# Attention and a mixture of experts on one core: order of the experts and the next weights' load ahead of the table, small copies and sums moved off GpSimd

## The chip, the core and the metric

The kernel runs on one core of a Trainium2 chip. The engines are called PE (TensorE), DVE (VectorE), ACT (ScalarE), POOL (GpSimd) and SP (SyncE, which here only issues transfers). The metric is the time on the device in microseconds; the kernel before took 555.93 us in the median of three runs (553.4 to 557.14).

## The reference

Attention with a capped score, then a layer of eight experts of which each token uses one:

```python
scores = cap * np.tanh(q @ k.T / np.sqrt(64) / cap)      # 4 batches, 12 heads, 448 tokens, 64 wide
attn = softmax(scores) @ v                               # becomes x: 1792 tokens of 768
logits = normalised(x) @ normalised(expert_emb).T / tau
expert_idx = np.argmax(logits, axis=1)
gate_w = softmax(logits)[token, expert_idx]
for e in range(8):                                       # w1[e]: 768 x 1024, w2[e]: 1024 x 768
    mask = expert_idx == e
    h = np.maximum(x[mask] @ w1[e], 0.0)
    out[mask] = gate_w[mask, None] * (h @ w2[e])
```

All arrays are float32. The kernel multiplies in float16 with each factor split into a high and a low half, three products for each pair.

## The kernel before, in words

The first part (up to about 250 us) is attention, head pair by head pair, with the router's work put between. Each batch's rows are written to a table of rows `x_dram` in device memory; each row has 768 values, then its scale and its gate, 770 words in all. The expert with the most tokens so far is chosen early; its weights are loaded and split beside attention, and its first tile (`tile0`) is computed from the rows of the first three batches.

The second part works in tiles of 128 tokens of one expert. `tile_body` does one: up products into `h` (12 groups, `up`, L231), `relu` into a high and a low half (`hh` on ACT at L243, `hl` on DVE at L244), eight down products (`down`, L638), and in between, after the sixth down product, the transposes of the next tile's rows (`transpose_x`, L212), which POOL gathered from `x_dram` (`gather`, L198) and scaled (`scale_x`, L204). A check sum of each low half's accumulator `acc` is added into `sum_h` by POOL (L653, in wide tiles L1399, for `tile0` L739). At the end of the kernel all sums are looked at (`fine_sums`, L1478 on).

Which tile belongs to which expert is computed on the chip. In the tile behind `tile0` (L1491) functions called hooks are run between the up groups, in the order of the dictionary `hooks1`: at group 0 `gates_out` (gates of the last batch, written to `x_dram` by two transfers of ACT's queue, L407 and L410) and `slots`; at group 8 `fill_table` (a product of PE, then DVE's `table`, L1213, then the gather of the next rows, which needs the table and the written gates), `positions` (the experts' order, as a permutation `perm`, and the list `by_pos` and `pos_i` by position in this order, L1220 to L1244) and `start_loads` (SP reads seven expert numbers from `pos_i` into registers, then loads the second expert's weights: six loads of `w1r` of 512 KB, L1153, and four of `w2r` of 768 KB, L1157); from group 10 on every engine reads registers from `pos_i` (`load_ends`).

Beside an expert's first tile the next expert's ten weight parts are split into halves, each by one ACT operation (L221) and one DVE operation (L222), and with each split the load of the part of the expert after that is issued (`load1`, `load2`). They stand in the queues of ACT and DVE between the `hh` and `hl` of that tile: four before the first half of the hidden layer, four before the second, the rest one by one (`FIRST`).

The experts at positions 1 to 4 have a first tile that is wide (`wide_tile`): 128 of their own tokens and 32 more, the tail of the expert. The 128 tail rows of these four are gathered together once (`along_gather`), scaled (`along_scale`, L1320), transposed beside the first tile of the largest expert (`along_transpose`, L1330 to L1333), and each expert's 32 columns are copied into columns 128 to 160 of `xh` and `xl` (`along_behind`, L1339, POOL, 6 x 32 words for each of the two).

The number of tiles of an expert is only known on the chip, so the tiles stand in branches (L1525 for further tiles of an expert, L1541 for the last experts). How the framework orders the engines: an engine's instructions run in the order of the program. Where one engine needs another's result, it waits for that engine's counting semaphore. At the end of a branch each engine raises its own semaphore to the value that it would have had in the other arm; an operation behind the branch that needs something which another engine wrote or read in the branch waits for this mark, which the other engine sets when it gets there itself. Each transfer that SP or ACT issues gets the next of eight semaphores, in the order of the program, whichever of the two issues it; before it is issued, its engine waits until the transfer that had this semaphore before, the eighth before it, has landed.

The functions concerned:

Of the kernel before, what the change touches and what calls it, by code (L numbers as in the profile page):

```python
# [30 lines left out]
F32 = mybir.dt.float32  # L31
F32R = mybir.dt.float32r
F16 = mybir.dt.float16
I32 = mybir.dt.int32
AF = mybir.ActivationFunctionType
ALU = mybir.AluOpType
AX = mybir.AxisListType
PSUM = bass.MemoryType.PSUM

P = 128  # L40
# [4 lines left out]
E = 8  # L45
# [8 lines left out]
TAIL = 32  # L54
# [26 lines left out]
def attention_moe(ctx: ExitStack, tc: tile.TileContext, q, k, v, cap, emb, tau, w1, w2, qk_pairs, v_pairs, out):  # L81
    nc = tc.nc
# [27 lines left out]
    iota_t = const.tile([P, NTAB], F32, name="iota_t")  # L110
    nc.gpsimd.iota(iota_t, pattern=[[1, NTAB]], base=0, channel_multiplier=0, allow_small_or_imprecise_dtypes=True)

    iota_e = const.tile([P, E], F32, name="iota_e")
# [70 lines left out]
    sums_w, sums_0, sum_h = sums[:, : E * NS], sums[:, E * NS : -3], sums[:, -3:]  # L184
# [4 lines left out]
    xh = const.tile([P, DC, PW], F16, name="xh")  # L189
# [80 lines left out]
    with ExitStack() as actx:  # L270
# [83 lines left out]
        def load_heads(i):  # L354
# [20 lines left out]
        halves, tails, done_full, place = [  # L375
            small.tile([P, E], F32, tag=n, name=n) for n in ("halves", "tails", "done_full", "place")
        ]
# [25 lines left out]
        def write_rows(b, c0, c1):  # L403

            for t in (b,) if b else (0, B - 1):
                eng = nc.sync if b < B - 1 else nc.scalar
                eng.dma_start(  # L407
                    x_dram[t * S : t * S + 384, c0:c1].rearrange("(p c) w -> p c w", c=3), xsb[b % 2][:, 0:3, c0:c1]
                )
                eng.dma_start(x_dram[t * S + 384 : (t + 1) * S, c0:c1], xsb[b % 2][: S - 384, 3, c0:c1])  # L410
# [19 lines left out]
        def gates_out(b):  # L430
            gs = small.tile([P, 4], F32, tag="gs", name=f"gs{b}")
            nc.vector.tensor_reduce(gs, ex, axis=AX.X, op=ALU.add)
            nc.vector.tensor_scalar(gs, gs, 1e-9, None, op0=ALU.add)
            nc.vector.reciprocal(gs, gs)
            nc.vector.tensor_tensor(xsb[b % 2][:, :, GATE], gs, p2, op=ALU.mult)
            write_rows(b, D, XW)
# [155 lines left out]
        def tile_body(p, idx, nxt, W=P, todo=(), pace=FIRST, hooks=(), hidden=None, space=None):  # L592
# [50 lines left out]
            if not hidden:  # L643
                hp = [tile_of("h", n) for n in range(2)]
                acc = small.tile([P, 2], F32, tag="acc", name="acc", bufs=2)
                hidden = []
                for h in range(2):
                    step(pace[h])
                    for j in range(DC):
                        hook(h * DC + j)  # L650
                        up(w1p[p % 2], h, j, hp[h], W)
                    hidden.append(relu(h, hp[h], acc, W))
                nc.gpsimd.tensor_tensor(sum_h[:, :2], sum_h[:, :2], acc, op=ALU.add)  # L653
            for f in range(6):
                hook(2 * DC + f)
                step(pace[2])
# [60 lines left out]
        acc0 = small.tile([P, 2], F32, tag="acc", name="acc0", bufs=2)  # L717

        last = B - 1
# [6 lines left out]
        def tile0(todo, space):  # L726

            todo = list(todo)

            def split_until(n):  # L730
                while len(todo) > n:
                    todo.pop(0)()

            hooks = {2 * DC + f: [lambda n=2 * (5 - f): split_until(n)] for f in range(6)}
            hooks[12] += [lambda: choose(last), lambda: all_norms(last)]
            hooks[15] += [count_last]
            hooks[16] += [lambda: scales_x(last), lambda: gates(last)]
            tile_body(0, idx0[:, 0:1], None, hooks=hooks, hidden=first_h, space=space)
            nc.gpsimd.tensor_tensor(sum_h[:, :2], sum_h[:, :2], acc0, op=ALU.add)  # L739

        def attention_bounded(apool, ps_s, ps_o):

# [391 lines left out]
    work = ctx.enter_context(tc.tile_pool(name="work", bufs=1))  # L1134
# [5 lines left out]
    raw2 = [wpool.tile([P, 2, D], F32, tag=f"w2r{f}", name=f"w2r{f}") for f in range(N2)]  # L1140


    NV = 6
    val = work.tile([P, NV, E], F32, tag="val", name="val")
    by_pos = work.tile([P, NV, E], F32, tag="by_pos", name="by_pos")
    pos_i = work.tile([1, 3, E], I32, name="pos_i")
    table = work.tile([P, NTAB], I32, name="table")
    cp = {}
    eid = {}
# [5 lines left out]
    def load2(p, f):  # L1155
        if p < E:
            nc.sync.dma_start(raw2[f], w2_part(eid[p], f))  # L1157
# [6 lines left out]
    def split2(p, f):  # L1164

        n = p * NS + N1 + f
        split(raw2[f], w2p[p % 2][0][f], w2p[p % 2][1][f], by_pos[:, 1, p : p + 1], sums_w[:, n : n + 1])
        load2(p + 1, f)

    def slots():  # L1170
        every = work.tile([P, E], F32, tag="every", name="every")
# [37 lines left out]
    def fill_table(start):  # L1209
        tp = ps_t.tile([P, 512], F32, tag="t", name="tabp")  # L1210
        for g in range(G):
            nc.tensor.matmul(tp[:, :NTAB], a_all[:, g, :], cp["b"][:, g, :], start=g == 0, stop=g == G - 1)
        nc.vector.tensor_scalar(table, tp[:, :NTAB], float(NT), None, op0=ALU.add)  # L1213
        gather(col(start))
        scale_x()
        gather(col(start + 1))

    def positions():

        nc.vector.tensor_copy(val[:, 0:2, :], scale_w)  # L1220
        nc.vector.tensor_copy(val[:, 2, :], unscale)

        nc.vector.scalar_tensor_tensor(
            out=val[:, 3, :], in0=full[:, 0, :], scalar=2.0, in1=halves, op0=ALU.mult, op1=ALU.add
        )

        nc.vector.tensor_tensor(val[:, 4, :], cp["t"], done, op=ALU.add)
        nc.vector.tensor_scalar(val[:, 5, :], iota_e, -1.0, float(E), op0=ALU.mult, op1=ALU.add)
        perm = work.tile([P, E, E], F32, tag="perm", name="perm")
        nc.vector.tensor_tensor(  # L1230
            perm,
            iota_t[:, :E].unsqueeze(2).to_broadcast([P, E, E]),
            place.unsqueeze(1).to_broadcast([P, E, E]),
            op=ALU.is_equal,
        )
        pv = work.tile([P, NV, E, E], F32, tag="pv", name="pv")
        nc.vector.tensor_tensor(
            pv,
            perm.unsqueeze(1).to_broadcast([P, NV, E, E]),
            val.unsqueeze(2).to_broadcast([P, NV, E, E]),  # L1240
            op=ALU.mult,
        )
        nc.vector.tensor_reduce(by_pos, pv, axis=AX.X, op=ALU.add)
        nc.vector.tensor_copy(pos_i, by_pos[0:1, 3:6, :])  # L1244

    def start_loads():
        for p in range(1, E):
            eid[p] = nc.values_load(
                pos_i[0:1, 2, p : p + 1], engines=(mybir.EngineType.SP,), min_val=0, max_val=E - 1
            )  # L1250
        for i in range(N1):
            load1(1, i)
        for f in range(N2):
            load2(1, f)
# [3 lines left out]
    def load_ends(p):  # L1258
# [4 lines left out]
        ends[p] = code, base  # L1263

    hooks1 = {
        0: [lambda: gates_out(last), slots],
        8: [lambda: fill_table(start), positions, start_loads],
        **{10 + i: [lambda i=i: load_ends(i)] for i in range(E)},
    }
    hooks1[10].append(lambda: along_gather())  # L1270
# [64 lines left out]
    def along_behind(p):  # L1335

        m = (p - WIDE.start) * TAIL
        for x, a in ((xh, along_h), (xl, along_l)):
            nc.gpsimd.tensor_copy(x[:, :, P:], a[:, :, m : m + TAIL])  # L1339

    def wide_tile(p, todo, pace=(4, 3, 3, 1)):

        code, base = ends[p]
        a = slice((p - WIDE.start) * TAIL, (p - WIDE.start + 1) * TAIL)
# [23 lines left out]
        acc = small.tile([P, 3], F32, tag="acc3", name="acc3")  # L1368
        hidden = {}
        for h in range(3):  # L1370
# [4 lines left out]
            for j in range(DC):  # L1375
                for f in fs:
                    c = slice(f * P, (f + 1) * P)
                    o = hp[:, (f - 3 * h) * PW : (f - 3 * h + 1) * PW]
                    for m, (l, x) in enumerate(((0, xh), (0, xl), (1, xh))):
                        nc.tensor.matmul(  # L1380
                            o, w1p[p % 2][l][j][:, c], x[:, j, :],
                            start=j == 0 and f == fs[0] and m == 0, stop=j == DC - 1 and f == fs[-1] and m == 2,
# [13 lines left out]
            )  # L1396
            for f in fs:
                hidden[f] = [t[:, (f - 3 * h) * PW : (f - 3 * h + 1) * PW] for t in parts]
        nc.gpsimd.tensor_tensor(sum_h, sum_h, acc, op=ALU.add)  # L1399
        y = [tile_of("y", n) for n in range(2)]  # L1400
        passes = ((0, 0), (0, 1), (1, 0))

# [17 lines left out]
        for f in range(FC):  # L1420
            for n, (l, w) in enumerate(passes):
                for m in range(blocks):
# [3 lines left out]
                        start=f == 0 and n == 0, stop=f == FC - 1 and n == 2, skip_group_check=True,  # L1426
# [21 lines left out]
    def tile_of(n, i):  # L1448
        if n == "o":
            return work.tile([P, D], F32, tag="yo", name="yo", bufs=2)  # L1450
        return ps.tile(shapes[n], F32, tag=f"{n}{i}", name=f"{n}{i}")
# [37 lines left out]
    with tc.manual_schedule():  # L1489
        start = nc.values_load(first_i[0:1, 1:2], engines=(mybir.EngineType.Pool,), min_val=0, max_val=2)  # L1490
# [65 lines left out]
        redo = nc.values_load(redo_i[0:1, 0:1], min_val=0, max_val=1)  # L1556
        with tc.If(redo > 0):
            for p in range(E):
                e = nc.values_load(pos_i[0:1, 2, p : p + 1], engines=(mybir.EngineType.SP,), min_val=0, max_val=E - 1)
                for i in range(N1):  # L1560
                    nc.sync.dma_start(raw1[i], w1_part(e, i))
                for f in range(N2):
                    nc.sync.dma_start(raw2[f], w2_part(e, f))
                n, base = ends[p]
                n = (n + 1) >> 1
                if p == 0:
                    n, base = n + nc.values_load(first_i[0:1, 1:2], min_val=0, max_val=2), 0
                with tc.For_i(0, n, 1) as slot:
                    plain_tile(base + slot)
                if p in WIDE:  # L1570
                    plain_tile(TAIL0 + p)
# [47 lines left out]
```

## Time and profile before

| | |
|---|---|
| time, median of 3 runs | 555.93 us (553.4 to 557.14) |
| the profiled execution | 559.05 us, span 557.2 us |
| PE busy | 485.3 us (87%) |
| DVE busy | 326.1 us (59%) |
| ACT busy | 299.9 us (54%) |
| POOL busy | 245.1 us (44%) |
| granted clock of PE, mean | 0.952 |

The span is the stretch from the first to the last instruction of the profiled execution; its own time is the device time around it. Busy shares are averages over attention and the experts. PE works on attention to about 246 us, and on tiles from then on. All times of rows are microseconds from the start of the span.

### The profile page before, as it was taken

What the parts mean: (1) busy time and instruction counts of PE and PEld (TensorE: products, weight loads), DVE (VectorE), ACT (ScalarE), POOL (GpSimd) and SP (SyncE); (2) the same over time, 40 slices, a digit from 0 to 9 for tenths busy, and PEclk for the clock granted to TensorE, in tenths of its full rate; (3) what the DMA queues carried; (4) which work ended last, traced back from release to release, by engine and by line L of the source; (5) the groups of instructions that cost most, each with busy time, mean ns of one, the idle gap of its engine ahead of it and who ended that gap; (6) DMA issues with size and microseconds to landing.
All of it is one profiled execution on the core that took longest, in us unless ns stands there. A gap on an engine that the chain in (4) does not pass through costs nothing. (4 is left out here: it accounts for less than half of the span.)

```text
span 557.2 us, 11978 instructions
## 1 busy us (share of the span) xinstructions
PE 485.3 (87%) x4603; PEld 314.2 (56%) x4603; DVE 326.1 (59%) x691; ACT 299.9 (54%) x366; POOL 245.1 (44%) x316
## 2 busy tenths in 40 slices
PE   3899989999997989798795996999999999989570
PEld 2444444444432434366683884987788877868450
DVE  4876686967897778677658213741218521869111
ACT  3988779788977987645055113711118311947010
POOL 2567636474634544720356333342125732463412
PEclk9999999999997979989997899999999999999776
DMA  7333318333262340342199810861115711679511
GB/s 227 120 108 111 110 43 265 108 110 106 103 223 80 144 155 1 113 129 90 60 351 407 322 58 20 288 229 43 41 59 214 304 58 59 225 297 349 199 32 39
DMA packets 30601, 83.55 MB, mean 150 GB/s; under 512 B 7293, under 2 KB 7449, under 8 KB 30498
## 3 DMA queue, kind: packets, MB, share of 16 engines
q1 hardware_dynamic: 26354, 67.68, 34.6%
q0 software_dynamic: 2896, 13.00, 6.9%
q10 hardware_dynamic: 1248, 1.64, 0.9%
q8 instruction: 47, 0.77, 0.6%
q14 instruction: 56, 0.46, 0.3%
HBM read 69.91 MB, written 13.00 MB: 149 GB/s over the span
## 5 line engine op out<-in xcount | busy, mean ns | idle before, releaser
L780 ACT ACTIVATE prob<-s,icap 128x896 f32<-128x896 f32 x96 | 86.2, 903 | 26.5 <-PE s L774 18.5
L231 PEld LDWEIGHTS <-h 128*128 128x128 f16 x1056 | 81.0, 100 | 13.6 <-ACTq L1541 7.2
L231 PE MATMUL h<-xh,h 128*128 128x128 f16 (+1 forms) x480 | 79.8, 220 | 9.5 <-ACTq L1541 6.8
L794 POOL TENSOR_TENSOR sums<-sums,prob 128x896 f32<-128x896 f32 x23 | 48.3, 2101 | 84.7 <-DVE sums L792 75.6
L784 ACT ACTIVATE prob<-prob,cap_b 128x896 f32<-128x896 f32 (+1 forms) x64 | 81.7, 1277 | 2.1
L231 PE MATMUL h<-xl,h 128*128 128x128 f16 (+1 forms) x480 | 79.8, 220 | 0.0
L231 PE MATMUL h<-xh,l 128*128 128x128 f16 (+1 forms) x480 | 79.8, 220 | 0.0
L811 PE MATMUL v<-prob,vb 128*64 128x448 f32 x288 | 72.1, 580 | 2.9 <-DVE xt L826 2.8
L800 POOL TENSOR_TENSOR sums<-sums,prob 64x448 f32<-64x448 f32 x47 | 63.8, 1358 | 3.6
L244 DVE SCALAR_TENSOR_TENSOR hl<-h,hh 128x512 f16<-128x512 f32 (+1 forms) x20 | 13.2, 663 | 72.4 <-ACT hh L243 55.3
L215 ACT CAST xh<-xt 128x384 f16<-128x384 f32 x32 | 13.9, 481 | 74.8 <-PE xt L212 60.7
L231 PEld LDWEIGHTS <-l 128*128 128x128 f16 x528 | 52.8, 100 | 0.0
L243 ACT ACTIVATE hh<-h 128x512 f16<-128x512 f32 (+1 forms) x20 | 11.5, 574 | 72.6 <-PE h L231 68.2
L774 PE MATMUL s<-hi 64*128 64x448 f32 x144 | 35.5, 483 | 14.8 <-DVE hi L756 12.4
L1380 PE MATMUL h<-xh,h 128*128 128x160 f16 x192 | 40.8, 236 | 8.4 <-POOLq L1525 4.2
L638 PEld LDWEIGHTS <-hh 128*128 128x128 f16 (+1 forms) x352 | 33.2, 102 | 23.0 <-ACT hh L243 3.3
L216 DVE TENSOR_TENSOR xl<-xt,xh 128x384 f16<-128x384 f32 x32 | 16.4, 551 | 50.8 <-ACT xh L215 50.7
L204 POOL TENSOR_TENSOR x_tile<-xg 128x768 f32<-128x768 f32 x17 | 26.3, 1549 | 44.0 <-PE xt L212 38.0
L638 PE MATMUL y<-h,hl 128*128 128x384 f16 (+1 forms) x160 | 39.5, 341 | 5.8 <-DVE hl L244 5.8
L222 DVE SCALAR_TENSOR_TENSOR l<-w1r,by_pos,h 128x1024 f16<-128x1024 f32 x30 | 37.3, 1291 | 10.5 <-ACT h L221 10.5
L638 PE MATMUL y<-h,hh 128*128 128x384 f16 (+1 forms) x160 | 39.2, 339 | 3.0 <-ACT hh L243 3.0
L774 PEld LDWEIGHTS s<-hi 64*128 64x128 f32 x144 | 14.4, 191 | 47.7 <-ACT prob L780 15.4
(307 smaller groups left out, 1133.4 us busy)
## 6 DMA issues: line engine op xcount, KB each, us to landing
w1r<-in_moe_w_dram SPq DMA_DIRECT2D x36, 512.0 KB, 6.5
w2r<-in_moe_w_dram SPq DMA_DIRECT2D x24, 768.0 KB, 8.3
qkb<-in_qk_pairs_dram SPq DMA_DIRECT2D x11, 960.0 KB, 5.6
vb<-in_v_pairs_dram SPq DMA_DIRECT2D x12, 512.0 KB, 6.3
x_dram<-xsb SPq DMA_DIRECT2D x4, 1152.0 KB, 5.9
ring<-in_moe_w_dram SPq DMA_DIRECT2D x6, 512.0 KB, 3.3
ring<-in_moe_w_dram SPq DMA_DIRECT2D x8, 384.0 KB, 3.1
x_dram<-xsb ACTq DMA_DIRECT2D x1, 1152.0 KB
```

Of the source, the lines that this page charges most:

```text
L204: nc.gpsimd.tensor_tensor(x_tile, xg[:, :D], xg[:, SCALE : SCALE + 1].to_broadcast([P, D]), op=ALU.mult)
L216: nc.vector.tensor_tensor(lo, t, hi, op=ALU.subtract)
L222: nc.vector.scalar_tensor_tensor(out=lo, in0=raw, scalar=scale, in1=hi, op0=ALU.mult, op1=ALU.subtract, accum_out=acc)
L231: nc.tensor.matmul(hp[:, f, :W], l[j][:, c], x[:, j, :W], start=j == 0 and f == 0 and n == 0, stop=j == DC - 1 and f == 3 and n == 2, skip ...
L638: nc.tensor.matmul(y, hidden[h][l][:, c, o : o + k], w2p[p % 2][w][f // 2][:, f % 2, m * C : (m + 1) * C], start=f == 0 and n == 0, stop=f ...
L774: nc.tensor.matmul(sp[:, s, :S], l[sl, kc], r[sl, :], start=n == 0, stop=n == 2)
L780: nc.scalar.activation(o, d, AF.Tanh, scale=icap)
L784: nc.scalar.activation(o, o, AF.Exp, scale=cap_b)
L794: nc.gpsimd.tensor_tensor(t, t, pt[:, 4:6, :], op=ALU.add)
L800: eng.tensor_tensor(t[sl, s, :], t[sl, s, :], pt[sl, 6, :], op=ALU.add)
L811: nc.tensor.matmul(o[s * DH : (s + 1) * DH, :S], vb[:, u, s * DH : (s + 1) * DH], pt[:, 2 * u + s, :], start=u == 0, stop=False, skip_grou ...
L1380: nc.tensor.matmul(o, w1p[p % 2][l][j][:, c], x[:, j, :], start=j == 0 and f == fs[0] and m == 0, stop=j == DC - 1 and f == fs[-1] and m == 2,
```

## The change

The order of the experts gets its own function `order` and its own small list `pos_e`; together with `start_loads` it is run at group 0, ahead of `gates_out` and `slots`, instead of behind `positions` at group 8. `positions` loses one of its six rows and the permutation. The columns of `along_behind` are copied by ACT (into `xh`) and DVE (into `xl`) instead of POOL. The three places that add check sums use DVE instead of POOL.

```diff
                     hidden.append(relu(h, hp[h], acc, W))
-                nc.gpsimd.tensor_tensor(sum_h[:, :2], sum_h[:, :2], acc, op=ALU.add)
+                nc.vector.tensor_tensor(sum_h[:, :2], sum_h[:, :2], acc, op=ALU.add)
...
             tile_body(0, idx0[:, 0:1], None, hooks=hooks, hidden=first_h, space=space)
-            nc.gpsimd.tensor_tensor(sum_h[:, :2], sum_h[:, :2], acc0, op=ALU.add)
+            nc.vector.tensor_tensor(sum_h[:, :2], sum_h[:, :2], acc0, op=ALU.add)
...
-    NV = 6
+    NV = 5
...
-    pos_i = work.tile([1, 3, E], I32, name="pos_i")
+    pos_i = work.tile([1, 2, E], I32, name="pos_i")
+    pos_e = work.tile([1, E], I32, name="pos_e")
+    perm = work.tile([P, E, E], F32, name="perm")
...
+    def order():
+
+        nc.vector.tensor_tensor(
+            perm,
+            iota_t[:, :E].unsqueeze(2).to_broadcast([P, E, E]),
+            place.unsqueeze(1).to_broadcast([P, E, E]),
+            op=ALU.is_equal,
+        )
+        which = work.tile([1, E, E], F32, tag="which_e", name="which_e")
+        nc.vector.tensor_tensor(which, perm[0:1], iota_t[0:1, :E].unsqueeze(1).to_broadcast([1, E, E]), op=ALU.mult)
+        with nc.allow_low_precision("numbers of experts, exact"):
+            nc.vector.tensor_reduce(pos_e, which, axis=AX.X, op=ALU.add)
...
         nc.vector.tensor_tensor(val[:, 4, :], cp["t"], done, op=ALU.add)
-        nc.vector.tensor_scalar(val[:, 5, :], iota_e, -1.0, float(E), op0=ALU.mult, op1=ALU.add)
-        perm = work.tile([P, E, E], F32, tag="perm", name="perm")
-        nc.vector.tensor_tensor(
...
-        nc.vector.tensor_copy(pos_i, by_pos[0:1, 3:6, :])
+        nc.vector.tensor_copy(pos_i, by_pos[0:1, 3:5, :])
...
             eid[p] = nc.values_load(
-                pos_i[0:1, 2, p : p + 1], engines=(mybir.EngineType.SP,), min_val=0, max_val=E - 1
+                pos_e[0:1, p : p + 1], engines=(mybir.EngineType.SP,), min_val=0, max_val=E - 1
             )
...
     hooks1 = {
-        0: [lambda: gates_out(last), slots],
-        8: [lambda: fill_table(start), positions, start_loads],
+        0: [order, start_loads, lambda: gates_out(last), slots],
+        8: [lambda: fill_table(start), positions],
...
         for x, a in ((xh, along_h), (xl, along_l)):
-            nc.gpsimd.tensor_copy(x[:, :, P:], a[:, :, m : m + TAIL])
+            eng = nc.scalar.copy if x is xh else nc.vector.tensor_copy
+            eng(x[:, :, P:], a[:, :, m : m + TAIL])
...
-        nc.gpsimd.tensor_tensor(sum_h, sum_h, acc, op=ALU.add)
+        nc.vector.tensor_tensor(sum_h, sum_h, acc, op=ALU.add)
```

## Rows read from the trace of the kernel before

**Rows 1.** Waits of PE from 240 us on (waited for: us, times, longest).
```profile
PE y L638 <- DVE hl L244: 5.8, 2, 3.9
PE h L1380 <- POOLq L1525: 4.2, 1, 4.2
```

**Rows 2.** Timeline of PE (start, busy us, operation, [idle before <- releaser]).
```profile
273.83 0.22 PE L231 MATMUL h<-xh,h 128*128 128x128 f16 x1 [1.27 <-DVE pos_i L1244]
...
281.01 0.82 PE L212 MATMUL xt<-ident,x_tile 128*128 128x128 f32 x6
...
283.62 0.22 PE L231 MATMUL h<-xh,h 128*128 128x128 f16 x1
...
298.69 0.50 PE L638 MATMUL y<-h,hh 128*128 128x384 f16 x2 [2.96 <-ACT hh L243]
...
301.39 0.82 PE L638 MATMUL y<-h,hl 128*128 128x384 f16 x2 [1.87 <-DVE hl L244]
...
310.63 0.22 PE L231 MATMUL h<-xh,h 128*128 128x128 f16 x1
```

**Rows 3.** Timeline of ACT, around the gate writes and in the tile with splits.
```profile
266.04 0.65 ACTq L410 DMA_DIRECT2D x_dram<-xsb  x1
267.35 0.60 ACT L243 ACTIVATE hh<-h 128x512 f16<-128x512 f32 x1 [4.33 <-DVE more L1183]
...
294.62 1.58 ACT L221 ACTIVATE h<-w2r,by_pos 128x1536 f16<-128x1536 f32 x1 [2.06 <-DMA w2r<-in_moe_w_dram]
```

**Rows 4.** Busy us by engine (x instructions), granted clock, DMA share, GB/s, of two stretches.
```profile
300.00:302.00 2.00, 0.61 (x2) 0.36 (x3) 2.00 (x5) 1.25 (x1) 0.59 (x1) 0.50 1.01 397
348.00:351.00 3.00, 2.99 (x25) 2.99 (x25) 2.96 (x6) 1.13 (x2) 2.98 (x4) 0.55 0.82 225
```

**Rows 5.** Timeline of PE at the start of the first and second wide tile.
```profile
348.01 0.29 PE L1380 MATMUL h<-xh,h 128*128 128x160 f16 x1 [4.22 <-POOLq L1525]
...
420.31 0.24 PE L1380 MATMUL h<-xh,h 128*128 128x160 f16 x1 [0.77 <-ACTq L1525]
```

**Rows 6.** Timeline of DVE, last half tile.
```profile
536.70 0.42 DVE L244 SCALAR_TENSOR_TENSOR hl<-h,hh 128x256 f16<-128x256 f32 x1 [17.13 <-POOLq L1541]
```

**Rows 7.** Timeline of DVE, around order and table.
```profile
264.61 0.19 DVE L432 TENSOR_REDUCE gs<-ex 128x4 f32<-128x32 f32 x1 [2.27 <-issue]
...
270.52 0.68 DVE L244 SCALAR_TENSOR_TENSOR hl<-h,hh 128x512 f16<-128x512 f32 x1
...
271.74 0.22 DVE L1230 TENSOR_TENSOR perm<-iota_t,place 128x64 f32<-128x64 f32 x1
...
273.17 0.17 DVE L1244 CAST pos_i<-by_pos 1x24 int32<-1x24 f32 x1
...
285.53 1.28 DVE L222 SCALAR_TENSOR_TENSOR l<-w1r,by_pos,h 128x1024 f16<-128x1024 f32 x1 [1.18 <-ACT h L221]
```

**Rows 8.** Timeline of SP's queue: the six loads of the second expert's w1.
```profile
277.96 4.22 SPq L1153 DMA_DIRECT2D w1r<-in_moe_w_dram  x6
```

**Rows 9.** Line L222: count, min/median/max ns, of one expert's splits.
```profile
L222 DVE SCALAR_TENSOR_TENSOR l<-w1r,by_pos,h x6: 1279/1280/1284, 421.8 to 428.4; 128x1024 f16<-128x1024 f32 x6
...
L222 DVE SCALAR_TENSOR_TENSOR l<-w2r,by_pos,h x4: 1814/1814/1816, 429.6 to 435.4; 128x1536 f16<-128x1536 f32 x4
```

**Rows 10.** Waits of SP's queue, 262 to 320 us (us, times, longest).
```profile
SPq L1153 <- DMA w2r<-in_moe_w_dram: 3.8, 2, 2.4
```

**Rows 11.** Line L1153, issue to landing: the first three w1r loads; the sixth.
```profile
DMA to landing us min/median/max: 3.9/5.1/7.4
...
DMA to landing us min/median/max: 9.4/9.4/9.4
```

**Rows 12.** Issue to landing: line L198, gathers, 270 to 320 us; L410, gate write.
```profile
DMA to landing us min/median/max: 3.9/6.2/8.1
...
DMA to landing us min/median/max: 3.5/3.5/3.5
```

**Rows 13.** Timeline of POOL: its last scaling.
```profile
542.49 1.47 POOL L204 TENSOR_TENSOR x_tile<-xg 128x768 f32<-128x768 f32 x1 [2.14 <-PE xt L212]
```

More of the change, by code (lines that the diff above doesn't have):

```diff
@@ L1227, in positions @@
         nc.vector.tensor_tensor(val[:, 4, :], cp["t"], done, op=ALU.add)
-        nc.vector.tensor_scalar(val[:, 5, :], iota_e, -1.0, float(E), op0=ALU.mult, op1=ALU.add)
-        perm = work.tile([P, E, E], F32, tag="perm", name="perm")
-        nc.vector.tensor_tensor(
[L1231 to L1235, printed above, removed]
         pv = work.tile([P, NV, E, E], F32, tag="pv", name="pv")
@@ L1558, in attention_moe @@
             for p in range(E):
-                e = nc.values_load(pos_i[0:1, 2, p : p + 1], engines=(mybir.EngineType.SP,), min_val=0, max_val=E - 1)
+                e = nc.values_load(pos_e[0:1, p : p + 1], engines=(mybir.EngineType.SP,), min_val=0, max_val=E - 1)
                 for i in range(N1):
```

## The prediction, made before the change was run

> **What bounds the kernel now.** I read the waits of TensorE from the router on (after 240 us), because TensorE works nearly without a pause there and its pauses are what a change can win. Two of them belong to work that the change touches [rows 1]. The first lies in the first tile of the largest expert that has weight splits among its work. TensorE stands before the down products for the halves of the hidden layer (at 298.69 and 301.39 [rows 2]), ScalarE is late with them because a split in its queue waits for a weight to land (at 294.62 [rows 3]), and TensorE then runs at 0.50 of its clock [rows 4]. That tile takes from 283.62 to 310.63 [rows 2], 27.0 us. The second is the start of the first wide tile, where TensorE waits for POOL's sequencer at the branch of L1525 [rows 5]. A third sits at the end: VectorE's split of the last half tile waits 17.13 us for POOL's sequencer at L1541 [rows 6].
>
> **Early loads: what they win.** `order` is three small operations; one such took 0.22, and I count 0.25 from one to the next [rows 7]. VectorE's first operation in this block starts at 264.61 [rows 7], so the order of experts is known at 265.36 instead of 273.34, the end of `pos_i` [rows 7]. SP reads seven registers first: 277.96 less 273.34 is 4.62 us [rows 7, 8]. The first load then starts at 269.98, 8.0 us earlier. The ten loads are worth twelve of 512 KB; at the pace worked out below the last lands at 269.98 + 3.9 + 11 x 1.44 = 289.7, before ScalarE needs any of them (the tile begins near 294.5). The tile is then set by VectorE. Its first split starts 1.9 us into the tile (285.53 less 283.62 [rows 2, 7]); six splits of 1.28, two of 1.81 [rows 9] and two `hl` of 0.69 [rows 7] put the second `hl` at 14.6; two more splits and 1.0 us for `along_l` (two of the 0.5 us conversions) at 19.2; the transposes need nearly all of it, say 18.9, and from them to the end of a tile it is 283.62 less 281.01, 2.6 us [rows 2]. So 21.5 us instead of 27.0: 5.5 us won. Bounds: 3 where TensorE's remaining pauses (about 1.5 us twice) still halve its clock, 7 where they vanish.
>
> **Early loads: what they cost.** `start_loads` now stands ahead of `gates_out`, and it moves ten transfers past ScalarE's two writes of the gates. Transfers of SP and ScalarE share eight semaphores in program order, and one waits until the eighth before it has landed. That this happens shows in SP's queue: loads of `w1r` waited 3.8 us for `w2r` to land, with which they share no data [rows 10]. Before, the two writes came first and found theirs free: 266.04 and 267.35 stand close behind each other [rows 3]. Now they are eleventh and twelfth, so they wait for the third and the fourth load. Behind them on ScalarE stands `hh` of this tile (L243), behind that on VectorE `hl`, the table and the positions, and behind these TensorE, whose register reads need `pos_i`, and POOL's first gather.
>
> When does the fourth load land? The first took 3.9 us, the sixth, issued at 281.85, 9.4 [rows 8, 11]: five landings in 9.35 us, with two gathers of 0.39 MB between them, each worth 0.75 of a load. 9.35 over 6.5 is 1.44 us for each. The fourth lands at 269.98 + 3.9 + 3 x 1.44 = 278.2. Bounds: 277.8 at the fastest pace of my rows (397 GB/s [rows 4], 1.32 us a load), 280.9 with the gathers' share and the late issues left in. By the Trainium skill, "DMA: Bandwidth & Descriptors", section Specifications, the fabric's ceiling is 435 GB/s; three loads of 512 KB would then take 3.6 us instead of 4.3 (an estimate), and the sum would come out 0.7 us lower; no row here reaches that rate over a whole load train.
>
> Then 0.65 to issue the second write, 0.60 for `hh` [rows 3], 0.69 for `hl` [rows 7]: 280.15. From the end of `hl` (271.21) to the end of `pos_i` (273.34) it took 2.13 [rows 7]; without `perm` (0.25), one value (0.07) and a sixth of two operations of 0.55 it is 1.6: 281.75. TensorE follows 0.49 later, as 273.83 follows 273.34 [rows 2, 7]: 282.25, 8.4 us late, after standing 9 us. After the standstills of the tile with splits the clock was halved over 300 to 302 [rows 4]; I take 5 us of it after the restart, 2.5 us lost, between 1.2 and 4.1. With 281.01 less 273.83, 7.18 us of work [rows 2], the transposes of the next tile come at 291.95, 10.9 us late. Their data: the gate write issued at 278.2 landed 3.5 us after its issue in a quiet queue [rows 12]; I stretch it as the gathers were, 6.2 over 3.9 [rows 12], to 5.6: 283.8. The gather takes 6.2 under load, the scaling 1.47 [rows 13]: 291.5. Both paths meet; TensorE's decides. Bounds: 9.2 us with the early landing and 1.2 us for the clock, 15.4 with the late landing and 4.1 or more. So this part costs 10.9 - 5.5 = 5.4 us.
>
> **Copies of the wide tiles' columns.** TensorE's first wide tile reads columns that POOL wrote inside the branch of the expert before it, and so waits for POOL's mark at the end of the branch, 4.22 us [rows 5]. With ScalarE and VectorE as writers, whose marks TensorE waits for anyway, the pause should be that of the second wide tile, 0.77 [rows 5]: 3.45 us. The half clock behind it, 0.55 over 348 to 351 [rows 4], goes with it: 3 x 0.45 = 1.3. Together 4.7 us; 3.4 if the clock falls all the same, nothing if another of POOL's values holds TensorE. The copies themselves (192 columns) lie on ScalarE and VectorE behind the last `hl` of a tile, under the last two down products (2 us); I cost them at nothing, at 0.4 us each time if that cover were gone.
>
> **Check sums on VectorE.** Five words for each tile; 0.2 us each, in pauses in which VectorE waits for the transposes. Nothing. But POOL read `acc` in the branches, and so VectorE's `hl` of the last half tile waited for POOL's mark [rows 6]. Without it TensorE's 3.9 us [rows 1] go, and what is late next is POOL itself, whose indices come when they came. Its scaling at 542.49 waited 2.14 us for TensorE's transposes [rows 13]; that wait goes, and POOL's last gather, which sets the end, comes 2.1 us earlier. Bounds: 0 and 3.9.
>
> **Sum.** +5.4 - 4.7 - 2.1 = -1.4 us. The profiled execution took 559.05, so 557.65; it stood 3.1 above the median of the runs, 555.93, so I forecast **554.5**. Own range of this case: from 9.2 - 7 - 4.7 - 3.9 = -6.4 to 15.4 - 3 - 3.4 - 0 = +9, both ends unlikely together; I keep -6 to +5.
>
> **Rivals.** (a) *The writes do not wait* (the semaphores fall another way): then only the first gather suffers, 2.3 us later under load against 3 us in hand, and 5.5 + 4.7 + 2.1 = 12 us are won: **543.6**. The wait between loads that share no data speaks against it [rows 10]. 0.13.
> (b) *Slower: the first gather's chain.* If the small gate write and the gather behind it land as the slowest gather did (8.1 [rows 12]; the write 7.3), and the fourth load at 280.9, the write lands at 288.2, the gather at 296.3, the rows are scaled at 297.8: 16.8 us late, with TensorE standing once more and a halved clock in the tile that follows, which leaves 2 of the 5.5 us. 16.8 - 2 - 6.8 = +8: **564**. It decides once the transposes come after 293.3 (6.8 + 5.5 behind 281.0), and is beyond 1% after 298.9. For it: slow landings [rows 12]; against it: the load is nearly over by then. By the Trainium skill, "DMA: Bandwidth & Descriptors", section Queues, rings and completion order, each DMA engine takes its queues in turn, packet by packet; by that rule a gather should not wait out a whole train of loads, which lowers this chance; the 6.2 against 3.9 agrees. 0.13.
> (c) *POOL still holds the first wide tile*: the 4.7 us stay, **559.2**. The wait's place speaks for POOL's writes alone as its cause. 0.05.
> The forecast has 0.69.
>
> A measurement of this kernel can tell about 1%, 5.6 us, from no change. Faster by that: rival (a), and 0.10 of the forecast's low end: 0.23. Slower by that: 0.10 from (b), 0.02 from the forecast's high end: 0.12. Within: 0.65. The range runs from the low end of the forecast to its high end with part of (b): 548.5 to 560.5; it leaves out (a) and the far part of (b).
>
> **What would show it.** The first load at 270; on ScalarE the second gate write only at about 278 with `hh` close behind it, and TensorE at rest from 273 to 282, with half its clock after it; transposes of the next tile near 292; the tile with splits in 21.5 us, no split waiting for a weight; the first wide tile starting 0.8 us after its predecessor; the last half tile without 3.9 us before its down products, and POOL's last scaling 2 us earlier beside TensorE's end. Wrong if the gate writes start near 266, if the tile with splits keeps its pauses, or if the first wide tile keeps a pause over 2 us.

## The result, and where the time went

The changed kernel took 548.7 us in the median (548.04 to 549.48, 4 runs), the kernel before 554.89 (553.4 to 557.14) beside it: a ratio of 0.9886, interval 0.9844 to 0.9927. Two later series, on two chips, gave 0.9915 (0.9886 to 0.9943) and 0.9905 (0.9874 to 0.9936). So it is about 1% faster. I had forecast 554.5, with 548.5 to 560.5 as the range: the time lies at the very edge of it, and the likeliest case did not happen. Rival (a) did, with less to win than I gave it. That the time still falls inside the range, by 0.2 us, is luck: of the two largest terms of the sum, the cost of 10.9 us did not appear and the gain of 5.5 came to nothing in the time, so that their errors nearly took each other away and 5.4 us were left. Without these 5.4 us the same sum gives 549.1.

First ScalarE's queue and TensorE in the changed kernel, from the router on (start, duration, operation, then the idle time before it and what ended it).

```profile
265.76 0.56 ACTq L407 DMA_DIRECT2D x_dram<-xsb  x1
266.35 1.21 ACTq L410 DMA_DIRECT2D x_dram<-xsb  x1
267.66 0.60 ACT L243 ACTIVATE hh<-h 128x512 f16<-128x512 f32 x1 [5.00 <-DVE both L1199]
```

```profile
262.71 0.22 PE L231 MATMUL h<-xh,h 128*128 128x128 f16 x1 [1.38 <-ACT x_tile L669]
...
273.77 0.22 PE L231 MATMUL h<-xh,h 128*128 128x128 f16 x1 [0.93 <-DVE by_pos L1250]
...
282.32 0.88 PE L212 MATMUL xt<-ident,x_tile 128*128 128x128 f32 x6 [1.19 <-POOL x_tile L204]
...
284.98 0.22 PE L231 MATMUL h<-xh,h 128*128 128x128 f16 x1
...
299.71 0.50 PE L638 MATMUL y<-h,hl 128*128 128x384 f16 x2 [1.98 <-DVE hl L244]
301.79 1.54 PE L1337 MATMUL along_t<-ident,room 128*128 128x128 f32 x6 [1.58 <-POOL room L1327]
...
305.76 1.54 PE L212 MATMUL xt<-ident,x_tile 128*128 128x128 f32 x6 [0.51 <-DVE along_l L1340]
...
323.01 0.82 PE L212 MATMUL xt<-ident,x_tile 128*128 128x128 f32 x6
...
339.51 0.82 PE L212 MATMUL xt<-ident,x_tile 128*128 128x128 f32 x6
...
343.38 0.23 PE L1388 MATMUL h<-xh,h 128*128 128x160 f16 x1 [1.11 <-ACTq L1533]
...
359.19 0.82 PE L212 MATMUL xt<-ident,x_tile 128*128 128x128 f32 x6
...
484.75 0.82 PE L212 MATMUL xt<-ident,x_tile 128*128 128x128 f32 x6
```

The gate writes go out at 265.76 and 266.35, where they did before [rows 3]; they wait for no load, TensorE is back at work at 273.77 (before 273.83 [rows 2]), and the 9 us standstill of my forecast is not there. The first load starts early, as forecast:

```profile
269.92 3.09 SPq L1155 DMA_DIRECT2D w1r<-in_moe_w_dram  x6
```

The transposes (L212) cut the time into stretches that can be compared between traces. I measure R1 from the first product behind the router (262.71 above) to the next transposes, R2 and R3 to the following ones (R2 is the tile with splits), "wide" over the start of the first wide tile (339.51 to 359.19), "tail" from 484.75 to the end of the span. The same marks in the kernel before:

```profile
263.07 0.22 PE L231 MATMUL h<-xh,h 128*128 128x128 f16 x1 [1.38 <-ACT x_tile L669]
...
306.33 1.54 PE L212 MATMUL xt<-ident,x_tile 128*128 128x128 f32 x6 [0.93 <-DVE along_l L1333]
...
341.02 0.82 PE L212 MATMUL xt<-ident,x_tile 128*128 128x128 f32 x6
...
365.09 0.82 PE L212 MATMUL xt<-ident,x_tile 128*128 128x128 f32 x6
```

With the transposes at 281.01 [rows 2], 324.52 and 490.68 they give the stretches of the table. The other stretches behind the router do not differ: from R3 to "wide" it is 16.5 us and from there to the tail 125.6 us in every trace. R1 itself begins between 259.6 and 267.2 us from trace to trace (262.7 to 267.2 for the changed kernel alone), because the attention ahead of it varies; in this pair that is 0.4 us.

| stretch, us | before | after |
|---|---|---|
| R1 | 17.94 | 19.61 |
| R2 | 25.32 | 23.45 |
| R3 | 18.19 | 17.25 |
| wide | 24.07 | 19.69 |
| tail | 66.57 | 62.93 |

These five differ by 9.2 us in favour of after. That is more than the medians show, in part because the profiled execution of before (559.05 us) stood 4 us above its median; so one pair of traces says where time went, but not how much, and the experiments below give every stretch several traces.

### The profile page after: what moved, and what is told of

It is laid out like the page before. It is cut to its first block, busy times and chain, and to the rows that moved or that the text cites. A ratio compares the mean times of both kernels' runs of the same rounds, so it can differ in the third digit from the quotient of the medians.

```text
span 547.7 us, 11970 instructions
## 1 busy us (share of the span) xinstructions
PE 480.5 (88%) x4603; PEld 311.4 (57%) x4603; DVE 330.8 (60%) x711; ACT 300.5 (55%) x370; POOL 245.8 (45%) x293
## 5 line engine op out<-in xcount | busy, mean ns | idle before, releaser
L780 ACT ACTIVATE prob<-s,icap 128x896 f32<-128x896 f32 x96 | 86.3, 904 | 25.8 <-PE s L774 16.6
L231 PE MATMUL h<-xh,h 128*128 128x128 f16 (+1 forms) x480 | 78.4, 218 | 9.3 <-SPq L1549 6.9
L231 PE MATMUL h<-xl,h 128*128 128x128 f16 (+1 forms) x480 | 78.4, 218 | 0.0
L231 PE MATMUL h<-xh,l 128*128 128x128 f16 (+1 forms) x480 | 78.4, 218 | 0.0
L222 DVE SCALAR_TENSOR_TENSOR l<-w1r,by_pos,h 128x1024 f16<-128x1024 f32 x30 | 37.7, 1305 | 8.8 <-ACT h L221 8.8
L774 PEld LDWEIGHTS s<-hi 64*128 64x128 f32 x144 | 14.4, 190 | 48.6 <-ACT prob L780 16.7
L1388 PE MATMUL h<-xh,l 128*128 128x160 f16 x192 | 39.9, 233 | 0.0
L1388 PE MATMUL h<-xl,h 128*128 128x160 f16 x192 | 39.9, 233 | 0.0
```

The source lines that it names most:

```text
L222: nc.vector.scalar_tensor_tensor(out=lo, in0=raw, scalar=scale, in1=hi, op0=ALU.mult, op1=ALU.subtract, accum_out=acc)
L231: nc.tensor.matmul(hp[:, f, :W], l[j][:, c], x[:, j, :W], start=j == 0 and f == 0 and n == 0, stop=j == DC - 1 and f == 3 and n == 2, skip ...
L774: nc.tensor.matmul(sp[:, s, :S], l[sl, kc], r[sl, :], start=n == 0, stop=n == 2)
L780: nc.scalar.activation(o, d, AF.Tanh, scale=icap)
L1388: nc.tensor.matmul(o, w1p[p % 2][l][j][:, c], x[:, j, :], start=j == 0 and f == fs[0] and m == 0, stop=j == DC - 1 and f == fs[-1] and m == 2,
```

## The experiments

All of them were run in three series, each beside the kernel before.

**The changed kernel again, and each part put back.** The first run is the base of its series.

> The changed kernel once more, as the base of the other three runs, and to see which of its times repeat. Theory A (from the two traces): the change won where the first wide tile starts (about 5 us) and at the end (3 to 4 us), and its early loads came out at about nothing, because what they win in the tile with splits (1.9 us) the first gather loses behind them (1.7 us). Rival B: the early loads won most of it, and the other two little. Both expect 548 to 550 here. In the profile A expects the first gather of the next tile 7 to 8 us from issue to landing and transposes L212 at 282 to 283, the second split tile's transposes at 305 to 306, the first wide tile 1.1 us behind its predecessor.

It took 553.12 us and not the 548 to 550 expected: this chip ran both kernels slower (before 558.15), so only the differences within the series count. Its stretches, R1 to tail: 19.60, 23.44, 16.69, 19.69, 61.77.

The loads late again, with columns and sums as changed:

```diff
-        0: [order, start_loads, lambda: gates_out(last), slots],
-        8: [lambda: fill_table(start), positions],
+        0: [lambda: gates_out(last), slots],
+        8: [lambda: fill_table(start), order, positions, order_e, start_loads],   # order_e: the sums of order
```

> The changed kernel with the order of experts taken after the table again (its matrix ahead of the positions, its sums behind them), so that the loads start when they did before; columns and sums stay as changed. Theory A: 548.5 to 550.5, within 1.5 us of the changed kernel: the first load at 278 again, the first gather back at about 4 us, the tile with splits back at 27 us. Rival B: 553 to 555, 5 us slower than the changed kernel.

It took 552.72 us, ratio 0.9911 (0.9875 to 0.9948): 0.4 under the changed kernel. In the tile with splits the stall of before is back.

```profile
PE y L638 <- ACT hh L243: 4.9, 1, 4.9
```

The first gather takes 3.8 us again. So the early loads as a whole are worth nothing that the times show, though this stall goes with them. Rival B falls.

Sums back on POOL:

```diff
-                nc.vector.tensor_tensor(sum_h[:, :2], sum_h[:, :2], acc, op=ALU.add)
+                nc.gpsimd.tensor_tensor(sum_h[:, :2], sum_h[:, :2], acc, op=ALU.add)     # and the other two
```

> The changed kernel with the three check sums back on POOL. Theory A: 551 to 553, 2 to 4 us slower, all of it in the last half tile, where VectorE's split waits for POOL's branch mark again and TensorE stands 3.9 us before its second half of down products; the tile with splits up to 1 us shorter, because the 2.07 us that the sum takes on VectorE there goes. Rival C: that 2.07 us in the tile with splits is worth as much as the end wins, so the time is the same within 1 us. Rival B: the same within 1 us as well, but with no gain in the tile with splits.

It took 554.94 us, 0.9928 (0.9893 to 0.9963): 1.8 above the changed kernel (2 to 4 expected), intervals overlapping, so the times alone do not show that the sums are worth anything. The traces do: the tail took 65.37 us, 3.6 more than in the changed kernel beside it, and the last half tile waits for POOL's mark again (two lines of DVE, the first for the tile with splits, then PE; compare [rows 6] and [rows 1]):

```profile
302.62 3.78 DVE L222 SCALAR_TENSOR_TENSOR l<-w2r,by_pos,h 128x1536 f16<-128x1536 f32 x1
...
533.40 0.42 DVE L244 SCALAR_TENSOR_TENSOR hl<-h,hh 128x256 f16<-128x256 f32 x1 [14.40 <-POOLq L1549]
```

```profile
533.89 0.35 PE L638 MATMUL y<-h,hl 128*64 128x384 f16 x2 [3.17 <-DVE hl L244]
```

The tile with splits did not get shorter (R2 23.31): where the check sum took 2.07 us in the changed kernel, now a split takes 3.78 instead of 1.81. Rival C falls; what stands behind those 2 us comes below.

Columns back on POOL:

```diff
-            eng = nc.scalar.copy if x is xh else nc.vector.tensor_copy
-            eng(x[:, :, P:], a[:, :, m : m + TAIL])
+            nc.gpsimd.tensor_copy(x[:, :, P:], a[:, :, m : m + TAIL])
```

> The changed kernel with the wide tiles' columns copied by POOL again. Theory A: 553 to 555, 4.7 to 5.5 us slower: TensorE waits 4.2 us for POOL before its first wide tile and runs some 3 us at half its clock behind it. Rival B, and the rival of the prediction in which something else of POOL holds that tile: 549 to 550, with TensorE's pause at that place under 2 us.

It took 557.61 us, 0.9985 (0.9952 to 1.0017): 4.5 above the changed kernel, and the pause of [rows 5] is back.

```profile
351.92 0.29 PE L1387 MATMUL h<-xh,h 128*128 128x160 f16 x1 [4.22 <-POOLq L1532]
```

**Does a write wait for a load?** My forecast's main cost did not appear. The built program shows why, and the traces, which keep each transfer's semaphore, agree: the eight semaphores of the hardware queues follow the order of the built program, which is not the order in which the code is written. The first four loads have numbers 0 to 3, the two gate writes 4 and 5, the other loads 6, 7, 0, 1, 2, 3. No load in flight holds 4 or 5. (Why the program is built in this order, no run shows.) Cutting the first write into five puts the last three of the six on 0, 1 and 2:

```diff
-                eng.dma_start(
-                    x_dram[t * S : t * S + 384, c0:c1].rearrange("(p c) w -> p c w", c=3), xsb[b % 2][:, 0:3, c0:c1]
-                )
+                q = 5 if (b == B - 1 and c0 == D) else 1
+                for k in range(q):
+                    a, z = k * P // q, (k + 1) * P // q
+                    eng.dma_start(
+                        x_dram[t * S + 3 * a : t * S + 3 * z, c0:c1].rearrange("(p c) w -> p c w", c=3),
+                        xsb[b % 2][a:z, 0:3, c0:c1],
+                    )
```

> The changed kernel with the first of the two gate writes cut into five by rows, so that the gates go out in six. Nothing else is new. In the program's list of semaphores the two writes of the changed kernel have the fifth and sixth of the eight that the hardware queues share, which no load in flight holds; with six writes the last three carry those of the first, second and third load. Theory A (a transfer waits until the one before it on its semaphore has landed): these three start on ScalarE only at about 273.5, 275.4 and 277.3 (when the loads landed in the changed kernel), hh at about 278 instead of 267.7, TensorE stands until 281 or 282, the next tile's transposes come 6 to 9 us later than in the changed kernel, and the time is 5 to 10 us above it: 0.3% to 1% above before. Rival D (writes never wait for loads on another queue): six writes end by 270, hh is hidden behind VectorE's work on the table, and the time is that of the changed kernel within 1 us.

It took 558.86 us, 1.006 (1.003 to 1.0091), where the changed kernel stands at 0.989 to 0.992 in its own three series (it was not run in this one). ScalarE's queue, then TensorE:

```profile
264.89 10.04 ACTq L410 DMA_DIRECT2D x_dram<-xsb  x5
276.09 0.51 ACTq L414 DMA_DIRECT2D x_dram<-xsb  x1
276.71 0.60 ACT L243 ACTIVATE hh<-h 128x512 f16<-128x512 f32 x1 [14.93 <-DMA w1r<-in_moe_w_dram]
```

```profile
280.19 0.26 PE L231 MATMUL h<-xh,h 128*128 128x128 f16 x1 [8.15 <-DVE pos_i L1255]
...
290.23 0.82 PE L212 MATMUL xt<-ident,x_tile 128*128 128x128 f32 x6
```

`hh` is held by a landing of `w1r`, with which it shares no data: the last three gate writes, ahead of it in ScalarE's queue, wait for the loads that had their semaphores. TensorE stands 8.15 us, and R1 is 28.40 us, 10.5 above before: the forecast had put 10.9 on just this chain. From its restart to the transposes TensorE took 10.04 us instead of 7.18, 2.9 lost where the forecast had 2.5, with its clock at 0.50 from 280 to 286. The mechanism and its price were right; that the changed kernel would run into it was wrong. Rival D falls.

**The early loads alone, on the kernel before.**

```diff
-        0: [lambda: gates_out(last), slots],
-        8: [lambda: fill_table(start), positions, start_loads],
+        0: [order, start_loads, lambda: gates_out(last), slots],
+        8: [lambda: fill_table(start), positions],
```

> The kernel before with the first part of the change alone: order and loads ahead, sums and columns on POOL. Theory A (the early loads win 1 to 2 us in the tile with splits beyond what the first gather loses): between 0 and 2 us faster than before, ratio 0.996 to 1.000. Rival B (they won 5 us): ratio 0.991. What the prediction forecast for this part (5.4 us slower) would be 1.010. In the profile A expects 19.6 us from the first product after the router to the next transposes (17.9 before) and 23 to 24 us from these to the transposes behind (25.3 before).

It took 556.94 us, 1.0024 (0.9994 to 1.0055). R1 is 20.20 and R2 23.31, near what Theory A had, yet nothing was won: the interval leaves a gain of 0.3 us at most and a loss of up to 3.1, and neither the 5.4 us of loss that I had forecast for this part (1.010) nor Rival B's gain (0.991) is there. The late loads once more, with the changed kernel and the kernel before beside them:

> The late loads once more, on another chip. Theory A (the early loads win at most 2 us): 0 to 2 us above the changed kernel. Theory F (they are worth nothing in the time, because what they take from the tile with splits the first gather gives back): within 1 us of it. Theory B (5 us) has fallen unless this run is 4 us or more above it.

> The changed kernel a third time, as the base of this call. 0.989 to 0.992 of the kernel before.

> The kernel before once more, for a second trace of it: which of its stretches repeat within 0.3 us, and which vary from run to run. Theory A: the first wide tile's start (24.1 us from the transposes ahead of it to the next) repeats, the stretch from the last wide tile to the end (66.6 us) varies by 1 to 3 us with the landing of the last loads, and so does the attention ahead of the router. Ratio 0.997 to 1.003.

Late loads 549.1 us (0.9886, 0.9845 to 0.9927), changed kernel 550.04 (0.9905), before again 555.62 (0.9993). So the two kernels can't be told apart here either, as Theory F had it. In the second trace of the kernel before, "wide" took 25.36 us where I had expected 24.1 to repeat; the tail took 66.01. The traces with late and early loads, sorted:

| | R1 | R2 | R3 | sum |
|---|---|---|---|---|
| late (before twice, late loads twice): mean | 18.16 | 25.80 | 17.17 | 61.13 |
| early (after three times, sums, columns, loads alone): mean | 19.87 | 23.41 | 17.89 | 61.17 |
| late: from, to | 17.94, 18.42 | 25.32, 26.83 | 16.68, 18.19 | 60.60, 61.85 |
| early: from, to | 19.60, 20.20 | 23.31, 23.52 | 16.69, 18.42 | 59.73, 62.03 |

The early loads win 2.4 us in the tile with splits, lose 1.7 in the tile ahead of it, and in the mean give the rest back in the tile behind it; but there the single traces of both kinds spread over the same range, so that this last loss is not shown. The first loss is the gather: it takes 7.6 to 8.2 us in the six early traces where it took 3.7 to 3.9 in the late ones [rows 12]. What moves R3 is TensorE's clock. One and the same work takes 16.7 to 18.4 us there. In the third run of the changed kernel TensorE paused 1.42 us before these transposes, and its clock behind was 0.50, the 1.2 GHz level; in the first run with late loads the pause was 0.20 and the clock 1.00, the 2.4 GHz level (windows: the start and end, busy time of the five engines, clock, share of the DMA engines, GB/s).

```profile
309.00:312.00 3.00, 2.91 (x11) 2.04 (x12) 1.83 (x5) 0.96 (x2) 1.28 (x1) 0.50 1.02 380
```

```profile
305.00:308.00 3.00, 2.93 (x21) 2.00 (x22) 1.73 (x6) 0.94 (x2) 1.59 (x2) 1.00 1.03 404
```

With early loads TensorE's waits in that tile (for `hl`, for the tails' rows, for `along_l`) stand close together at its end, right before R3; with late loads the long wait for `hh` stands 6 to 8 us before it. That this order brings the lower level into R3 more often (over 18 us in four of six traces with early loads, in one of four with late) is argued from few traces, not shown. The pause right before does not decide it alone: in the second trace of the kernel before TensorE paused 1.52 us there, and its clock behind was 1.00 and R3 16.69. No run changed the pause alone.

**Two attempts at more.** Seven of the ten loads behind the first gather:

```diff
-        for i in range(N1):
+        for i in range(3):
             load1(1, i)
-        for f in range(N2):
-            load2(1, f)
+    def rest_loads():                      # at group 8, behind positions
+        pos_r = work.tile([1, 1], I32, name="pos_r")
+        nc.vector.tensor_copy(pos_r, pos_e[0:1, 1:2])
...                                         # register from pos_r, then the other seven loads
```

> The changed kernel with only three loads ahead of the table; the other seven wait for a number that VectorE copies behind the positions, so they start about 1.5 us behind the first gather's issue instead of ahead of it. If it is the loads in flight that stretch the first gather (7.7 us instead of 3.9), the gather lands 1 to 2 us earlier, the 1 us pause of TensorE before the next tile's transposes goes, and the time is 0.5 to 1.5 us under the changed kernel; the last weights still land before ScalarE needs them. If the gather is stretched by something else, it takes over 7 us again and the time does not move. If the seven loads come too late, ScalarE waits for a weight in the tile with splits and the time is 1 to 3 us above the changed kernel.

It took 549.24 us (0.9872, 0.9834 to 0.9909). Issue to landing of the first gather (shortest, median, longest), first in the changed kernel, then here:

```profile
DMA to landing us min/median/max: 7.7/7.7/7.7
```

```profile
DMA to landing us min/median/max: 5.1/5.1/5.1
```

So it is the loads in flight that stretch it. TensorE's pause ahead of the transposes is gone and R1 is 18.54, but R3 took 18.38; the ratio can't be told from the changed kernel's (0.9886 to 0.9915 in its own three series). And POOL's scaling of the tails' rows one tile earlier:

```diff
+    hooks1[17].append(lambda: along_scale())
-                        hooks |= {2: [along_scale], 2 * DC + 5: [along_transpose, lambda: along_behind(1)]}
+                        hooks |= {2 * DC + 5: [along_transpose, lambda: along_behind(1)]}
```

> The changed kernel with POOL's scaling of the tails' rows (1.47 us) put one tile earlier, ahead of its scaling of the next tile's rows. In the changed kernel this scaling ran from 300.27 to 301.74, and VectorE's check sum, issued at 299.69 and 0.16 us long elsewhere, ended with it at 301.76. Theory A (the two engines exclude each other there): the check sum takes under 0.3 us, TensorE's 1.6 us pause before the tails' transposes goes, and the tile with splits is 1 to 2 us shorter; POOL's scaling now holds up a split of VectorE earlier in the tile by up to 1.5 us instead, which may take the gain back. Rival E (the check sum is slow there for a reason of its own): it stays near 2 us.

It took 549.99 us (0.9897, 0.9852 to 0.9942); R2 is 22.73, 0.7 us shorter and not the 1 to 2 expected. A split and the check sum of VectorE, then POOL's next scaling:

```profile
294.50 3.01 DVE L222 SCALAR_TENSOR_TENSOR l<-w2r,by_pos,h 128x1536 f16<-128x1536 f32 x1
...
298.16 0.16 DVE L653 TENSOR_TENSOR sums<-sums,acc 128x2 f32<-128x2 f32 x1
```

```profile
292.83 3.06 POOL L204 TENSOR_TENSOR x_tile<-xg 128x768 f32<-128x768 f32 x1
```

The check sum is down to 0.16 us and TensorE's pause before the tails' transposes is gone, so Theory A holds there and Rival E falls; the exclusion now falls on a split (3.01 us) and on POOL's next scaling (3.06), as that line allowed, and TensorE's wait for the second `hl` grew from 1.98 to 3.07 us. Together:

> The changed kernel with the two edits that each shortened their stretch: seven of the ten loads behind the first gather, and POOL's scaling of the tails' rows one tile earlier. If the stretches add, 18.5 us from the first product behind the router to the next transposes and 22.7 us from these to the next (19.6 and 23.4 in the changed kernel), 1.7 us together, so 1.5 to 2.5 us under the changed kernel in this call. If the pauses only move (a later gather, a later split), within 1 us of it.

550.28 us (0.9924, 0.9895 to 0.9953): no gain over the changed kernel beside it. R1 18.60 and R2 22.62 are 1.1 and 0.8 us shorter, as expected; TensorE still paused before R3, which took 18.19. No version was shown to beat the changed kernel.

## Why the prediction was right or wrong

- **What the loads cost, +10.9: the step that failed.** "Now they are eleventh and twelfth" is wrong: it counts in the order of the code, and the semaphores follow that of the built program. There the writes are fifth and sixth and wait for no load; R1 grew by 1.7 (19.87 against 18.16) instead of 10.9, and that is the gather behind the loads, not the writes. With six writes the forecast's own chain appeared, at 10.5.
- **What the loads win, -5.5: too large.** The second `hl` ended at 299.66, 14.7 us into the tile (14.6 forecast). The transposes came at 20.8 instead of 18.9, about the 1.9 us by which the check sum, costed at 0.2 us, took longer (2.07) while POOL scaled the tails' rows. And 1.7 of the 5.5 was the slow end of the old tile (4.3 us from transposes to end against 2.6 [rows 2]), which comes back in R3 in most traces with early loads. What is left is the 1.9 of this pair, 2.4 in the mean.
- **Rival (a)** had the first gather 2.3 us later with 3 us in hand. It took 3.8 us longer to land, and TensorE waited 1.19 for its rows. With the full 5.5 in it the rival gave 543.6, 5 us too little.
- **Columns, -4.7: right.** The first wide tile starts 1.11 us after its predecessor (0.8 forecast) and the clock stays up (1.00 over 343 to 346; 0.55 behind the pause of before [rows 4]): "wide" takes 19.7 us in all ten traces with the columns on ScalarE and VectorE, 24.1 to 25.4 in the four with POOL's: 4.8 in the mean, 4.5 by the medians.
- **Sums, -2.1: right in what waits, and of about the size.** VectorE's two halves are split as they come, and POOL is late next, as forecast:

```profile
523.58 0.42 DVE L244 SCALAR_TENSOR_TENSOR hl<-h,hh 128x256 f16<-128x256 f32 x1 [10.41 <-ACT hh L243]
...
525.68 0.43 DVE L244 SCALAR_TENSOR_TENSOR hl<-h,hh 128x256 f16<-128x256 f32 x1 [1.67 <-ACT hh L243]
```

```profile
532.28 1.47 POOL L204 TENSOR_TENSOR x_tile<-xg 128x768 f32<-128x768 f32 x1
```

  POOL's last scaling moved up 3.9 us against the start of the half tile (12.7 us behind it; before 542.49 less 525.89, 16.6). The tail takes 63.5 us in the mean of ten traces with sums on DVE (61.8 to 65.8) and 66.4 of four with sums on POOL (65.4 to 67.5): 2.9; 1.8 by the medians, whose intervals overlap. That POOL's scaling would come earlier beside TensorE's end was wrong: TensorE's last down product ended at 530.12, 2.2 us ahead of it, because TensorE won more than POOL did.

So of the 5 to 6 us most are the columns' (4.5 by the medians, clear of the noise) and the rest the sums' (about 2). Their two stretches add to 7.7 us, more than the whole; where the difference goes is open. The part that stands first in the change's name, the order and the loads ahead of the table, is worth nothing here that the times show.

## What to carry to other kernels

Before a transfer is moved past others, read in the built program which semaphore each gets: a write that shares one with a load in flight holds up all that stands behind it in its engine's queue, and the order in the code does not tell. A small helper can cost most through what waits for its engine's mark at a branch; here moving it to engines that are waited for anyway won more than its own time. What a transfer started earlier wins must be set against what it slows: here a 0.39 MB gather behind 3 MB of loads.

## What the runs showed of the hardware

VectorE and POOL shut each other out in some pairs of operations. In the changed kernel (VectorE, then POOL):

```profile
291.72 0.69 DVE L244 SCALAR_TENSOR_TENSOR hl<-h,hh 128x512 f16<-128x512 f32 x1
...
292.33 2.02 DVE L222 SCALAR_TENSOR_TENSOR l<-w1r,by_pos,h 128x1024 f16<-128x1024 f32 x1
...
299.69 2.07 DVE L653 TENSOR_TENSOR sums<-sums,acc 128x2 f32<-128x2 f32 x1
```

```profile
291.81 1.46 POOL L204 TENSOR_TENSOR x_tile<-xg 128x768 f32<-128x768 f32 x1
...
300.27 1.47 POOL L1327 TENSOR_TENSOR room<-room 128x768 f32<-128x768 f32 x1
301.68 0.18 POOL L1330 COPY along_g<-room 128x1 f32<-128x1 f32 x1
301.80 1.73 POOL L217 COPY gates<-gates 128x1 f32<-128x1 f32 x1
```

The check sum (0.16 us elsewhere) ends with POOL's scaling, at 301.76 and 301.74, and in the run with that scaling moved away it took 0.16. A split that meets a scaling takes 2.02 instead of 1.28, and a POOL copy of 0.2 us that meets a split takes 1.73. `hl`, which reads PSUM and one tile, runs beside POOL's scaling at its full speed (0.69). The Trainium skill, "SBUF — State Buffer", section "SBUF: two separate sides", says that a VectorE operation with two SBUF inputs and a GpSimd operation that reads SBUF lock each other out for the whole instruction; these rows agree that they wait for each other. Which of the two goes first they do not show: the check sum is recorded from 299.69, 0.58 us before the scaling, and still ended with it.
